# The last 64 tokens of v on 64 partitions, their weights transposed by TensorE

## The chip, the core and the metric

The kernel runs on one core of a Trainium2 chip. The metric is the device time of one execution in microseconds (us), as the median of several runs. The engines are TensorE (PE, with its weight loads shown apart as PEld), VectorE (DVE), ScalarE (ACT), GpSimd (POOL) and SyncE (SP), which issues nearly all transfers.

## The reference, cut to what matters

There are 8 batches of 8 heads, 576 tokens and a head size of 64. For each head 32 packed queries `p` attend to all 576 keys `k` and values `v`; the packed result then serves as keys and values for the 576 real queries. Two expert layers follow on 4608 tokens (512 to 1536 to 512, then 512 to 1024 to 1024 to 512), all in 32-bit floats.

```python
def sm_attn(qq, kk, vv):
    s = scale * np.matmul(qq, kk.transpose(0, 1, 3, 2))
    s = s - np.max(s, axis=-1, keepdims=True)
    a = np.exp(s)
    a = a / (np.sum(a, axis=-1, keepdims=True) + 1e-09)
    return np.matmul(a, vv)
p_packed = sm_attn(p, k, v)
out = sm_attn(q, p_packed, p_packed)
```

The change touches the first of the two calls alone, in its last part: exp, the transposes of its result (the weights of the sum over tokens), and the product with `v`.

## The kernel before, in words

The first call is worked in 16 units. Unit `u` is four heads of one batch, so that its 4 x 32 packed queries fill 128 partitions. The work of a unit is spread over four steps of a loop that runs by hand-written order (line 625): in step `s` the kernel transposes the keys of unit `s` (`pa_kT`), makes the scores of unit `s - 1` (`pa_s`) and their exp (`pa_exp`), transposes the exp of unit `s - 2` (`pa_T`), multiplies it by `v` for unit `s - 3` (`pa_P`), and transposes the finished result of unit `s - 4` (`pa_PT`). Every engine takes its instructions in this order. Between them stand, at chosen quarter steps, the first pieces of the second call (`q_rows` to `q_aT`), of the weight conversion (`w_conv`, `raw_load`) and of the first expert layer (`c_mm`, `stage1`). From line 897 on the expert layers follow, in which TensorE works almost without a break.

The 576 tokens of `v` are taken in two parts. The first 512 (`TM`) come in one transfer for each unit, four neighbouring tokens to a partition (`vm`, line 497), so that partition `p` holds tokens `4 p` to `4 p + 3`. The last 64 (`TR`) come for four units at once (`load_vr`, line 480), in four transfers, one for each head of a unit: head `hq` lies on partitions `32 hq` to `32 hq + 31`, two neighbouring tokens to a partition.

The scores lie in PSUM as 2 x 288: the even tokens in the first half, the odd ones in the second, and in each half in an order that comes from the transposes of the keys. `pa_exp` reads them so and writes `a` as 2 x 288, in order of tokens within each half. `pa_T` picks for `r` from 0 to 3 every second element of a half (`a[:, r % 2, r // 2:256:2]`), which are the tokens `4 p + r`, and TensorE transposes these 128 columns as the weights of an identity product; ACT copies the four results out of PSUM into `apT`. The weights of the last 64 tokens are transposed by DVE, in blocks of 32 x 32 (`apR`, line 548). `pa_P` then sums in one PSUM tile: 16 products over 128 rows, with four heads side by side in four column groups of 32, and after them 8 products over 32 rows, in which head `hq` takes row group and column group `hq`. Line 575 scales the sum by the reciprocal of the exp's sum.

PSUM tiles of two banks (`psum`) go round in three buffers; SP issues the transfers in program order, and an issue waits where its buffer isn't free.

Of the kernel before, what the change touches and what calls it, by code (L numbers as in the profile page):

```python
# [8 lines left out]
F32 = mybir.dt.float32  # L9
# [29 lines left out]
def packed_attention_moe_kernel(  # L39
# [24 lines left out]
    nc = tc.nc  # L64
    B, H, S, D = q.shape
# [4 lines left out]
    HS = S // 2  # L70
    NR = S // 32
    TR = 64
    TM = S - TR
    NV = TM // 128
# [9 lines left out]
    def pool(name, side, bufs=1, **kw):  # L84
        return tc.alloc_tile_pool(name=name, bufs=bufs, side=side, reuse_waits="tile", **kw)
# [25 lines left out]
    ident = const.tile([128, 128], F32, name="ident")  # L111
# [15 lines left out]
    def psum(name):  # L127
        ps_n[0] += 1
        return ps_at[ps_n[0] % len(ps_at)].tile([128, 2, 512], F32, tag="A", name=name)

    def psum1(name):
        return psB.tile([128, 512], F32, tag="B", name=name)
# [4 lines left out]
    hs = [slice(32 * hq, 32 * hq + 32) for hq in range(4)]  # L137
# [329 lines left out]
    pa = pool("pa", "left", bufs=2)  # L467
# [7 lines left out]
    def twice_p(b0, b1):  # L475
        nc.gpsimd.tensor_copy(zp[:, b0:b1, :, 1], zp[:, b0:b1, :, 0])

    vr = pa.tile([128, 2 * B, 2 * D], F32, tag="vr", name="vr", bufs=1)

    def load_vr(u0, u1):  # L480
        for hq in range(4):
            nc.sync.dma_start(
                vr[hs[hq], u0:u1],
                v[u0 // 2:u1 // 2, :, TM:S].rearrange("b (q h) (p r) d -> h p (b q) (r d)", h=4, r=2)[hq])

    def load_k(u):
        if not 0 <= u < 2 * B:
# [46 lines left out]
        return t, mx  # L534

    def pa_exp(u, t, mx):
        a = pa.tile([128, 2, HS], F32, tag="ap", name=f"ap{u}")
        sm = pa.tile([128, 1], F32, tag="sm", name=f"sm{u}", bufs=3)
        nc.scalar.activation(
            a.rearrange("j e (p m) -> j e p m", m=NR // 2),  # L540
            t[:, :, 0:HS].rearrange("j e (m p) -> j e p m", m=NR // 2),
            AF.Exp, bias=mx, scale=scale, accum_out=sm)
        ap_t[u], sm_t[u] = a, sm

    def pa_T(u):
        a, sm = ap_t.pop(u), sm_t[u]
        aR = pa.tile([128, 2, 32], F32, tag="apR", name=f"apR{u}")
        nc.vector.transpose(out=aR, in_=a[:, :, 256:HS])
        nc.vector.tensor_scalar(sm, sm, 1e-9, None, op0=ALU.add)
        nc.vector.reciprocal(sm, sm)  # L550
        t = psum(f"pat{u}")[:, 0]
        for r in range(NV):
            nc.tensor.transpose(
                t[:, 128 * r:128 * r + 128], a[:, r % 2, r // 2:256:2], ident)
        aT = pa.tile([128, NV, 128], F32, tag="apT", name=f"apT{u}")
        pin_at["act"] = nc.scalar.copy(aT, t.rearrange("p (r n) -> p r n", r=NV))
        apT_t[u] = aT, aR

    def pa_P(u):
        vm = kv.pop(("v", u))  # L560
        aT, aR = apT_t.pop(u)
        sm = sm_t.pop(u)
        t = psum1(f"pP{u}")
        for r in range(NV):
            for hq in range(4):
                nc.tensor.matmul(
                    t[hs[hq], 0:64], lhsT=aT[:, r, hs[hq]], rhs=vm[:, hq, D * r:D * r + D],
                    start=(r == 0), stop=False, tile_position=(0, 32 * hq))
        for r in range(2):
            for hq in range(4):  # L570
                nc.tensor.matmul(
                    t[hs[hq], 0:64], lhsT=aR[hs[hq], r], rhs=vr[hs[hq], u, D * r:D * r + D],
                    start=False, stop=(r == 1), tile_position=(32 * hq, 32 * hq))
        Pd = pa.tile([128, 2, 64], F32, tag="Pd", name=f"Pd{u}")
        pin_at["dve"] = nc.vector.tensor_scalar(
            Pd, t[:, 0:64].rearrange("p (o d) -> p o d", o=1).to_broadcast([128, 2, 64]), sm, None, op0=ALU.mult)
        Pd_t[u] = Pd
# [46 lines left out]
    with tc.manual_schedule(engines=M0):  # L624
        for s in range(last + 1):
            if s < U:
                pa_kT(s)
            load_v(s - VD)
            if s == 0 or (s % 4 == 3 and s + 1 < U):
                load_vr(s + (s > 0), s + (s > 0) + 4)  # L630
            load_k(s + KVB)
            run(s, 0)
            run(s, 0.25)
            if 0 <= s - 1 < U:
                x = pa_s(s - 1)
            if 0 <= s - 4 < U:
                pa_PT(s - 4)
            run(s, 0.5)
            if 0 <= s - 2 < U:
                pa_T(s - 2)  # L640
            if 0 <= s - 1 < U:
                pa_exp(s - 1, *x)
            if 0 <= s - 3 < U:
                pa_P(s - 3)
            run(s, 0.75)
# [677 lines left out]
```

## Time and profile before

| what | value |
|---|---|
| timed runs | median 1349.32 us of 3 (1349.02 to 1351.62) |
| the profiled execution | 1353.27 us, of which 1351.4 us are the span from its first to its last instruction |
| busy share of the span | PE 98%, PEld 93%, DVE 54%, ACT 45%, POOL 35% |
| TensorE's granted clock | 0.999 of full, over the span |
| moved by DMA | 278.32 MB, 206 GB/s on average |

The times of the rows further down are those of the profiled execution. A busy TensorE is not TensorE at its peak, because products overlap: the pace of a run of products is read from the length of the run, less that of its last one, divided by their number less one. A wait is put down to the event that ended it.

### The profile page before, as it was taken

The page shows a single profiled execution, that of the slowest core. Times are in us where ns is not written, and L with a number is a line of the kernel's source. Part 1 is how long each engine was busy: PE and PEld are TensorE (multiplying, and loading weights), DVE is VectorE, ACT ScalarE, POOL GpSimd, SP SyncE. Part 2 cuts the span into 40 slices and gives each one's busy share as a digit, 9 for nine tenths or more (in the row PEclk, how much of TensorE's full clock was granted, in tenths as well). Part 3 has the DMA queues.
Part 4 walks back from the last instruction along what each step waited for, and adds up shares of the span by engine and source line. Part 5 has one row for each costly group of instructions (what it writes and reads, how often), then busy time and mean ns, then how long its engine had stood idle before and what let it go on. Part 6 is the DMA issues. An engine that isn't in the chain of part 4 may idle for free.

```text
span 1351.4 us, 26602 instructions
## 1 busy us (share of the span) xinstructions
PE 1328.3 (98%) x10628; PEld 1252.2 (93%) x10628; DVE 731.2 (54%) x1114; ACT 607.6 (45%) x1068; POOL 467.0 (35%) x385
## 2 busy tenths in 40 slices
PE   8889999999999999999999999999999999999999
PEld 6679899999999999999999999889899999999999
DVE  4766877336564466544453389626535535456352
ACT  5774644244443444345554246434344334345241
POOL 1332322323322333244444236305225145153261
PEclk9999999999999999999999999999999999999999
DMA  9976766524445443243453249849769987978855
GB/s 315 343 238 209 214 200 191 168 74 130 148 129 180 121 128 126 71 148 120 142 153 117 81 162 337 292 151 346 250 226 309 313 296 269 318 258 277 315 203 172
DMA packets 192348, 278.32 MB, mean 206 GB/s; under 512 B 71008, under 2 KB 124256, under 8 KB 189920
## 3 DMA queue, kind: packets, MB, share of 16 engines
q1 hardware_dynamic: 192224, 276.62, 63.0%
q8 instruction: 84, 1.38, 0.4%
q14 instruction: 40, 0.33, 0.1%
HBM read 217.84 MB, written 58.72 MB: 205 GB/s over the span
## 4 chain that ended last, share of the span: by engine, by line
PE 81%; DMA 4%; DVE 3%; ACT 1%; issue 0%; SPq 0%; DVEq 0%; ACTq 0%
PE px L675 20%; PE pA L1111 14%; PE pg L446 10%; PE pv L446 9%; PE pB L1111 7%; PE po L1201 5%; PE poA L1225 4%; PE pC L1111 3%; PE pw L767 3%; PE poB L1225 3%; PE pc L413 2%; DMA x2r<-X2d 1%; DMA out_dram<-kA 1%; PE psq L210 1%; DVE x2T L843 1%
## 5 line engine op out<-in xcount | busy, mean ns | idle before, releaser
L89 POOL TENSOR_TENSOR ul<-u,uh 128x576 fp32r<-128x576 f32 x96 | 145.9, 1520 | 303.8 <-ACT uh L96 281.9
L675 PE MATMUL px<-uh,woh 128*128 128x384 f32 x576 | 147.7, 337 | 0.2
L675 PE MATMUL px<-ul,woh 128*128 128x384 f32 x576 | 146.3, 334 | 0.0
L675 PE MATMUL px<-uh,wol 128*128 128x384 f32 x576 | 146.3, 334 | 0.0
L455 DVE TENSOR_TENSOR u<-u,pv 128x576 f32<-128x576 f32 x96 | 71.9, 750 | 135.3 <-PE pv L446 119.3
L687 DVE TENSOR_TENSOR acc<-acc,px 128x768 f32<-128x768 f32 x72 | 68.1, 950 | 85.1 <-PE px L675 84.6
L96 ACT CAST uh<-u 128x576 fp32r<-128x576 f32 x96 | 64.6, 674 | 103.5 <-DVE u L455 103.1
L89 POOL TENSOR_TENSOR wol<-wof,woh 128x512 fp32r<-128x512 f32 x48 | 65.3, 1370 | 126.7 <-ACT woh L96 121.6
L675 PEld LDWEIGHTS px<-uh,woh 128*128 128x128 f32 x576 | 102.5, 188 | 6.0 <-issue 3.3
L451 ACT ACTIVATE u<-pg 128x576 f32<-128x576 f32 x96 | 62.6, 652 | 96.6 <-PE pg L446 90.7
L675 PEld LDWEIGHTS px<-uh,wol 128*128 128x128 f32 x576 | 104.1, 188 | 0.0
L675 PEld LDWEIGHTS px<-ul,woh 128*128 128x128 f32 x576 | 104.1, 188 | 0.0
L446 PE MATMUL pg<-aTh,ch 128*128 128x288 f32 x384 | 83.9, 300 | 1.2 <-DVE cl L89 0.8
L446 PE MATMUL pv<-aTh,ch 128*128 128x288 f32 x384 | 82.8, 297 | 0.9 <-DVE cl L89 0.6
L446 PE MATMUL pg<-aTh,cl 128*128 128x288 f32 x384 | 82.3, 296 | 0.5 <-DVE cl L89 0.5
L446 PE MATMUL pg<-aTl,ch 128*128 128x288 f32 x384 | 82.4, 296 | 0.0
L446 PE MATMUL pv<-aTh,cl 128*128 128x288 f32 x384 | 82.1, 295 | 0.0
L446 PE MATMUL pv<-aTl,ch 128*128 128x288 f32 x384 | 82.1, 295 | 0.0
L446 PEld LDWEIGHTS pg<-aTh,ch 128*128 128x128 f32 x384 | 63.0, 188 | 9.3 <-DVE u L455 3.2
L89 DVE TENSOR_TENSOR cl<-pc,ch 128x1024 fp32r<-128x1024 f32 x48 | 56.6, 1216 | 26.2 <-ACT ch L425 26.2
L446 PEld LDWEIGHTS pv<-aTh,ch 128*128 128x128 f32 x384 | 61.7, 188 | 2.0 <-DVE cl L89 0.8
L446 PEld LDWEIGHTS pg<-aTh,cl 128*128 128x128 f32 x384 | 61.9, 189 | 0.7 <-DVE cl L89 0.7
(415 smaller groups left out, 3443.5 us busy)
## 6 DMA issues: line engine op xcount, KB each, us to landing
wsp<-wsd SPq DMA_DIRECT2D x112, 512.0 KB, 4.3
wf<-Wd SPq DMA_DIRECT2D x36, 512.0 KB, 5.7
wob<-wobd SPq DMA_DIRECT2D x18, 1024.0 KB, 7.1
wsd<-ws SPq DMA_DIRECT2D x56, 256.0 KB, 3.2
ws<-wsd SPq DMA_DIRECT2D x49, 256.0 KB, 5.2
wob<-wobd SPq DMA_DIRECT2D x40, 256.0 KB, 5.6
km<-in_k_dram SPq DMA_DIRECT2D x16, 576.0 KB, 7.3
wof<-wod SPq DMA_DIRECT2D x36, 256.0 KB, 2.8
```

Source lines behind the costliest of these rows:

```text
L89: x = eng.tensor_tensor(out=out, in0=src, in1=hi.bitcast(F32), op=ALU.subtract)
L96: nc.scalar.copy(hi, src)
L413: nc.tensor.matmul(t[hs[at], b, Q], lhsT=PTd[es, 2 * (2 * P + b) + Q, hs[hq]], rhs=w[es, 2 * Q + hq // 2].rearrange("p g n -> p (g n)"), s ...
L446: nc.tensor.matmul(t[:, hf, 0:HS], lhsT=w[:, b % 2, Q, cols], rhs=x[:, Q, hf, :], start=first, stop=last,)
L451: x = nc.scalar.activation(u, t[:, :, 0:HS], AF.Silu)
L455: x = nc.vector.tensor_tensor(out=u, in0=u, in1=t[:, :, 0:HS], op=ALU.mult)
L675: nc.tensor.matmul(t[:, h, 0:CW], lhsT=w[:, 128 * d:128 * d + 128], rhs=x[:, CW * c:CW * c + CW], start=first, stop=last,)
L687: pin_at["acc"] = nc.vector.tensor_tensor(out=o, in0=o, in1=t[:, :, 0:CW], op=ALU.add)
L767: nc.tensor.matmul(t[:, 1], lhsT=a[:, kk], rhs=w, start=(i == 0), stop=(i == 11))
L1111: nc.tensor.matmul(bk[n], lhsT=w[:, hl, 128 * d:128 * d + 128], rhs=r[:, d], start=(first and d == 0 and i == 0), stop=(d == 1 and i == 2) ...
L1201: nc.tensor.matmul(t, lhsT=a[:, j, cols], rhs=w[:, f], start=first, stop=last)
L1225: nc.tensor.matmul(bk[n][m], lhsT=l, rhs=w[i][:, h], start=(first and i == 0 and q == 0), stop=(i == NPB - 1 and q == 2), skip_group_check ...
```

## The change

The last 64 tokens of `v` come in one transfer for four units instead of four: 64 partitions, one token to a partition, all heads beside each other. Exp writes `a` as one row of 576 in order of tokens, so that even tokens are written in steps of two elements, and odd ones likewise. The four sources of TensorE's transposes are then `a[:, r:512:4]`, and the last 64 columns are a fifth source, transposed by TensorE into the second bank of the same PSUM tile and copied out by DVE, where DVE made the transpose itself. The 8 products over 32 rows become 4 over 64 rows, all on the first 64 rows of the array, one for each column group.

```diff
-    vr = pa.tile([128, 2 * B, 2 * D], F32, tag="vr", name="vr", bufs=1)
+    vr = pa.tile([TR, 8 * B, D], F32, tag="vr", name="vr", bufs=1)
     def load_vr(u0, u1):
-        for hq in range(4):
-            nc.sync.dma_start(
-                vr[hs[hq], u0:u1],
-                v[u0 // 2:u1 // 2, :, TM:S].rearrange("b (q h) (p r) d -> h p (b q) (r d)", h=4, r=2)[hq])
+        nc.sync.dma_start(
+            vr[:, 4 * u0:4 * u1], v[u0 // 2:u1 // 2, :, TM:S].rearrange("b h p d -> p (b h) d"))
...
-        a = pa.tile([128, 2, HS], F32, tag="ap", name=f"ap{u}")
+        a = pa.tile([128, S], F32, tag="ap", name=f"ap{u}")
...
-            a.rearrange("j e (p m) -> j e p m", m=NR // 2),
+            a.rearrange("j (p m e) -> j e p m", m=NR // 2, e=2),
...
-        aR = pa.tile([128, 2, 32], F32, tag="apR", name=f"apR{u}")
-        nc.vector.transpose(out=aR, in_=a[:, :, 256:HS])
...
-        t = psum(f"pat{u}")[:, 0]
+        t2 = psum(f"pat{u}")
+        t = t2[:, 0]
         for r in range(NV):
             nc.tensor.transpose(
-                t[:, 128 * r:128 * r + 128], a[:, r % 2, r // 2:256:2], ident)
+                t[:, 128 * r:128 * r + 128], a[:, r:TM:NV], ident)
+        nc.tensor.transpose(t2[0:TR, 1, 0:128], a[:, TM:S], ident)
+        aR = pa.tile([TR, 128], F32, tag="apR", name=f"apR{u}")
+        nc.vector.tensor_copy(aR, t2[0:TR, 1, 0:128])
...
-        for r in range(2):
-            for hq in range(4):
-                nc.tensor.matmul(
-                    t[hs[hq], 0:64], lhsT=aR[hs[hq], r], rhs=vr[hs[hq], u, D * r:D * r + D],
-                    start=False, stop=(r == 1), tile_position=(32 * hq, 32 * hq))
+        for hq in range(4):
+            nc.tensor.matmul(
+                t[hs[hq], 0:64], lhsT=aR[:, hs[hq]], rhs=vr[:, 4 * u + hq],
+                start=False, stop=True, tile_position=(0, 32 * hq))
```

## Rows read from the trace of the kernel before

**Rows 1.** The page, parts 1 and 4: busy time; the chain's shares by engine.

```profile
PE 1328.3 (98%) x10628; PEld 1252.2 (93%) x10628; DVE 731.2 (54%) x1114; ACT 607.6 (45%) x1068; POOL 467.0 (35%) x385
...
PE 81%; DMA 4%; DVE 3%; ACT 1%; issue 0%; SPq 0%; DVEq 0%; ACTq 0%
```

**Rows 2.** Windows: length, then busy us of PE, PEld, DVE, ACT, POOL; clock; DMA.

```profile
12.00:86.00 74.00, 66.88 (x1320) 47.59 (x1322) 52.40 (x141) 56.88 (x109) 18.43 (x14) 1.00 1.00 320
86.00:150.00 64.00, 62.65 (x638) 56.33 (x635) 40.95 (x63) 38.04 (x57) 20.29 (x14) 1.00 0.68 206
150.00:770.00 620.00, 618.52 (x5119) 586.14 (x5118) 328.89 (x418) 267.22 (x381) 216.39 (x150) 1.00 0.46 137
```

**Rows 3.** Waits of PE, 12 to 95 us: sum, times, longest (us).

```profile
PE pPT L581 <- DVE Pd L575: 1.4, 1, 1.4
PE pP L566 <- ACT kT L516: 1.2, 2, 0.8
PE pkr L514 <- issue: 1.0, 1, 1.0
PE pat L553 <- DVE qT L180: 0.8, 2, 0.6
PE pg L446 <- DVE cl L89: 0.8, 1, 0.8
PE pP L566 <- issue: 0.6, 1, 0.6
```

**Rows 4.** Timeline of PE, 36 to 46 us: start, length (us), instructions merged.

```profile
38.08 0.64 PE L553 MATMUL pat<-ident,ap 128*128 128x128 f32 x4
38.65 0.65 PE L566 MATMUL pP<-vm,apT 128*32 128x64 f32 x32
39.23 0.42 PE L571 MATMUL pP<-vr,apR 32*32 32x64 f32 x16
39.59 1.09 PE L511 MATMUL pk<-ident,km 128*128 128x128 f32 x8
...
41.96 1.06 PE L177 MATMUL pqT<-ident,qr 128*128 128x128 f32 x8
```

**Rows 5.** Weight loads of two lines: ns min/median/max, first and last start (us).

```profile
L553 PEld LDWEIGHTS pat<-ident,ap x64: 194/207/218, 13.1 to 85.5; 128*128 128x128 f32 x64
...
L511 PEld LDWEIGHTS pk<-ident,km x128: 137/141/231, 5.4 to 74.4; 128*128 128x128 f32 x128
```

**Rows 6.** ACT's groups by form, whole span: busy us, mean ns, idle before.

```profile
L96 ACT CAST uh<-u 128x576 fp32r<-128x576 f32 x96 | 64.6, 674 | 103.5 <-DVE u L455 103.1
...
L96 ACT CAST woh<-wof 128x512 fp32r<-128x512 f32 x48 | 29.6, 620 | 72.2 <-PE px L675 50.7 <-DVE wof L354 15.2 <-DMA wof<-wod 6.1
...
L350 ACT ACTIVATE wf<-raw_w 128x512 f32<-128x512 f32 x24 | 15.4, 676 | 2.5 <-DMA raw_w<-in_moe_w_gate_dram 2.5
...
L539 ACT ACTIVATE ap<-psp,mx 128x576 f32<-128x576 f32 x16 | 11.9, 746 | 5.0 <-DVE mx L533 3.6 <-PE pk L511 1.4
...
L96 ACT CAST w3h(0, 0)_7494<-w3T(0, 0)_7492 128x512 fp32r<-128x512 f32 x1 | 1.2, 1165 | 0.7 <-DVE w3T(0, 0)_7492 L750 0.7
```

**Rows 7.** Groups by form, 0 to 95 us: busy us, mean ns, idle before.

```profile
L96 ACT CAST aTh<-aT 128x576 fp32r<-128x576 f32 x4 | 5.1, 1286 | 0.0
...
L548 DVE STREAM_TRANSPOSE apR<-ap 128x64 f32<-128x64 f32 x16 | 3.8, 235 | 0.0
...
L181 DVE COPY qT<-pqr 128x128 f32<-128x128 f32 x4 | 1.1, 280 | 0.0
```

**Rows 8.** DMA, 0 to 110 us: queue's packets, MB, share; issues, KB, us to landing.

```profile
q1 hardware_dynamic: 27280, 31.27, 89.8%
...
vr<-in_v_dram SPq DMA_DIRECT2D x16, 64.0 KB, 7.9
```

**Rows 9.** Timeline of SP, 53 to 60 us.

```profile
54.16 4.53 SPq L482 DMA_DIRECT2D vr<-in_v_dram  x4
```

**Rows 10.** Waits of ACT, 12 to 95 us: sum, times, longest (us).

```profile
ACT wf L350 <- DMA raw_w<-in_moe_w_gate_dram: 2.5, 1, 2.5
```

## The prediction

> **What bounds the kernel now.** I read the page's busy shares first: TensorE is busy for 98% of the span, and the chain that ended last is 81% TensorE [rows 1]. The view by windows then splits the span. From 150 to 770 us TensorE stands still for 1.5 us in 620; between 12 and 86 us, where the sixteen units of the packed attention run, it is busy 66.88 of 74 us, ACT 56.88, DVE 52.40, and the DMA engines are full (share 1.00) [rows 2]. So what the change does to these 74 us moves everything behind them, and what it does to TensorE there is the first thing to count: only 74 - 66.88 = 7.1 us of idle time can swallow it. The view of waits says how that idle time is cut up: six kinds of wait with a longest one of 0.6 to 1.4 us, ended by DVE, ACT or issue [rows 3]. None of the six is ended by a DMA.
>
> **The change part by part**, per unit, then times 16.
>
> *Products over the last tokens.* Eight products become four. Each stands in the trace as two records, four column groups running side by side, so 16 records are 4 rounds and become 2. The 32 records before them make 8 rounds: (0.65 - 0.22) / 7 = 0.061 us a round; the rounds to be cut give (0.42 - 0.21) / 3 = 0.07 [rows 4]. I take 2 x 0.061 = 0.12 us, 2.0 us in all; bounds 2.2 us saved and nothing saved (should the entry into the 64-row shape cost more than the one into the 32-row shape: entry now takes about 0.15 us against a round of 0.061: the last of the eight rounds begins at 38.65 + 7 x 0.061 = 39.08, the next at 39.23 [rows 4]).
>
> *One more transpose.* Its source, the last 64 columns, is contiguous. Contiguous 128-column transposes follow each other at (1.06 - 0.27) / 7 = 0.113 us [rows 4]; 16 of them are +1.8 us. Below: half of it, for 64 columns (0.9). Above: 0.113 and a change of array shape, 0.15 - 0.06 = 0.09 more (3.3).
>
> *The other four transposes.* Exp now writes in token order, so their sources step by four floats (16 bytes) where they stepped by two (8 bytes). This is the one large unknown, for no weight load of the trace steps that far. What it shows: the load of a contiguous 128-column block takes 141 ns, at 8-byte steps 207 ns [rows 5], and four such transposes follow each other at (0.64 - 0.28) / 3 = 0.12 us, or 0.94 ns a column [rows 4]. ACT shows farther steps. Its contiguous casts take 674 ns for 576 elements and 620 for 512, so (674 - 620) / 64 = 0.84 ns an element and 190 ns beside; the cast that reads in 512-byte steps takes 1165 ns, (1165 - 190) / 512 = 1.90 an element; the activation that reads every second word (8-byte steps) 676 ns, 0.95 [rows 6]; the cast that writes in 72-byte steps 1286 ns, again (1286 - 190) / 576 = 1.90 [rows 7]. Far steps cost 1.90, 8-byte steps half of that, on ACT as on the weight load (0.94). At 16 bytes the price is therefore between 0.94 (nothing added) and 1.90. I take 1.90: contiguous to 8 bytes has already lengthened the load, and another halving of the density lands on the far end. A transpose then comes every 1.90 x 128 = 0.24 us, 0.12 more than now; 64 of them are +7.7 us. Bounds: 0, and 0.24 + 0.11 = 0.35 us each if load and product stop overlapping (+14.7).
>
> The Trainium skill, "SBUF — State Buffer", section "Specifications (TRN2)", has 16-byte lines that want two hits each for full speed; two floats 8 bytes apart share a line and two 16 bytes apart don't, which is the price taken (the trace agrees on ACT's far steps, 1.90 against 0.84). But the same page, section "Door 1: The DMA port swizzle", says of stepping for free: "4 fp32". And "TensorE: Matmul & The Clock Gate", section "LDWEIGHTS (loading the stationary operand)", makes the load a matter of columns alone, about 107 ns for 128; the trace's 141 and 207 for the same 128 columns don't agree. By either sentence this edit costs nothing and the time is that of rival B.
>
> *DVE.* A 235 ns transpose goes, a copy out of PSUM comes: the 128x128 one takes 280 ns [rows 7], so +0.045 us a unit, 0.7 us in all, on an engine idle for a fifth of the stretch: nothing. The copy now waits for the fifth transpose, and behind it on DVE stands the scaling of the unit before, which waits for products that TensorE makes after these transposes anyway; the products that read the copy come a step later. Cover gone: 0.28 us a unit, 4.5 us. ACT's copy of the weights may wait for the fifth transpose too, 0.11 us, counted above.
>
> *Exp.* Writes in 8-byte steps: by the 0.95 above at most 0.11 x 576 = 0.06 us on 746 ns [rows 6], 1.0 us over 16 on an ACT with 17 us idle; I let 0.3 us through. Bounds: 0, and as the 72-byte write, (1.90 - 0.84) x 576 = 0.61 us each, 9.8 us on ACT.
>
> *Loads.* Four transfers become one, four times. The bytes stay (16 x 64 KB), the pieces go from 512 to 256 bytes. A vr transfer takes 7.9 us to land in a full queue [rows 8]; no wait of TensorE in [rows 3] is for one. I cost the transfer at nothing, with bounds in C and E below. On SP twelve issues go; four of them held it 4.53 us [rows 9], but what is behind them are loads of k and raw weights, and the only long DMA wait in the stretch is one of ACT, 2.5 us [rows 10].
>
> *Sum.* TensorE: 7.7 + 1.8 - 2.0 = +7.5 us, 0.47 a unit. How much of it reaches the end? The waits of [rows 3] are ended by ACT or DVE work that itself follows TensorE's work of the step before, so most idle time moves along; a wait can swallow one step's 0.47 us only if it is longer, and six such kinds are there: 6 x 0.47 = 2.8. Through come 7.5 - 2.8 = 4.7, with exp's 0.3 makes 5.0 us. The bounds of this step are 0.4 (all 7.1 us of idle time used) and 7.5. The profiled execution took 1353.27 us (span 1351.4 and 1.9 around it), 3.9 above the median of the timed runs; it would become 1358.3, the median 1349.3 + 5.0 = 1354.3 us.
>
> **The rivals.**
> A (forecast): the 16-byte step doubles the load. 1354.3, own range +2.5 to +7.7: 1351.8 to 1357.0.
> B: the step costs nothing, the load still hides at 0.12 us. TensorE gets 1.8 - 2.0 = -0.2 us: 1349.1, between -1.3 and +1.3. For it: 8-byte steps moved the pace of the transposes only from 0.113 to 0.12 us [rows 4], and if words are fetched in pairs, a 16-byte step fetches no more than an 8-byte one. Against it: ACT's 1.90 at far steps, twice its 0.95.
> C, the other side: faster. Place: SP's queue from 54.16 us on. With B's transposes (at best 0.9 - 2.0 = -1.1 us) and three of four issues gone (4.53 us become about 1.1), the raw weights start some 3 us sooner and ACT's wait of 2.5 us for them vanishes: -1.1 - 2.5 = -3.6, 1345.7. It decides only if that wait holds TensorE up; against it stands that none of TensorE's six is ended by a DMA.
> D: exp's writes cost as the 72-byte ones, 9.8 us on ACT, which has 17.1 us idle; with A's 5.0 and some 4 us of it showing, 1358.3. For it: the 72-byte write is the only strided write of ACT among the rows; against it: 0.95 at 8-byte reads.
> E: the queue. 1.05 MB of vr, at 31.27 MB in 89.8% of 110 us [rows 8], is 3.3 us of the queue; twice that if the halved pieces go at half the rate, +3.3 us on what waits for loads, with A 1357.6. Against it: no wait of TensorE on a DMA.
>
> **How the numbers follow.** A 0.58, B 0.20, C 0.12, D 0.06, E 0.04. What a measurement of this kernel can tell from no change is about 0.2%, 2.7 us. Slower by more: nearly all of A (0.54), D and E: 0.64. Within: the rest of A, B, a little of C: 0.26. Faster: 0.10. The range takes in A and B with its lower bound, and D and E in their middle: 1348.0 to 1358.5; left out are most of C, the upper ends of D and E, and the end of A's price where nothing overlaps.
>
> **What would show it.** Right: weight loads of pat at 300 ns or more, and four strided transposes spaced 0.24 us; the last unit's group, at 85.5 us now [rows 5], starting 4 to 5 us later, and the first products of the next stage as much later; the rounds over the last tokens two instead of four. Wrong: transposes still 0.12 us apart (then B); exp above 0.85 us (D); TensorE waiting for k, v or the last tokens of v (E). If the transposes do take 0.24 us but the stretch ends less than 2 us later, the step that fails is the share let through.

## The result, and the profile after

| | median | runs | ratio to before, 95% interval |
|---|---|---|---|
| before | 1349.17 us | 4 (1348.68 to 1351.62) | |
| after | 1359.95 us | 4 (1358.40 to 1361.45) | 1.0077 [1.0062, 1.0092] |

By the ratio the change costs 0.77%, 10.4 us; the two medians differ by 10.8. The profiled execution of after took 1358.40 us (span 1356.6), only 5.1 us more than that of before. The two profiles differ by more than that where the change is. First line L350's conversions of raw weights on ACT (duration in ns min/median/max, first and last start), before and then after:

```profile
L350 ACT ACTIVATE wf<-raw_w x24: 654/674/707, 50.4 to 201.1; 128x512 f32<-128x512 f32 x24
...
L350 ACT ACTIVATE vt_w<-raw_w x16: 657/669/697, 592.0 to 735.4; 128x512 f32<-128x512 f32 x16
```

```profile
L350 ACT ACTIVATE wf<-raw_w x24: 664/674/713, 52.4 to 211.6; 128x512 f32<-128x512 f32 x24
...
L350 ACT ACTIVATE vt_w<-raw_w x16: 661/672/707, 602.4 to 745.8; 128x512 f32<-128x512 f32 x16
```

At 201 us after is 10.5 us behind, at 735 us 10.4: all is lost in the packed attention and what overlaps it, nothing in the 500 us behind it. What the profile of before lost later is its own: from 870 to 880 us its clock is 0.83 (in after it is full there), and from 1050 to 1110 us its TensorE stands still for 2.26 of 60 us, where after has no idle time. By windows (length, then busy us of PE, PEld, DVE, ACT, POOL; granted clock; DMA share; GB/s), before and then after:

```profile
1050.00:1110.00 60.00, 57.74 (x411) 57.27 (x410) 28.12 (x47) 21.87 (x47) 14.93 (x15) 1.00 0.89 306
```

```profile
1050.00:1110.00 60.00, 60.00 (x427) 60.00 (x426) 29.06 (x48) 22.75 (x48) 17.11 (x18) 1.00 0.92 323
```

So I read the mechanism in the first 100 us and take the sizes from the timed runs. The windows of after that answer to the first two of [rows 2], and three short ones:

```profile
12.00:86.00 74.00, 63.03 (x1090) 44.00 (x1089) 47.56 (x130) 48.77 (x96) 15.20 (x12) 0.93 1.01 308
86.00:150.00 64.00, 58.89 (x609) 51.18 (x615) 38.54 (x60) 34.91 (x56) 18.91 (x13) 0.95 0.63 187
```

```profile
50.00:60.00 10.00, 7.50 (x121) 4.86 (x121) 7.18 (x16) 5.36 (x10) 2.89 (x2) 0.66 1.06 372
70.00:80.00 10.00, 6.91 (x84) 5.01 (x84) 6.69 (x16) 5.80 (x10) 1.75 (x1) 0.83 0.88 288
90.00:100.00 10.00, 7.53 (x114) 6.03 (x106) 3.98 (x10) 4.36 (x9) 0.79 (x1) 0.66 0.33 82
```

Every engine is less busy between 12 and 86 us than before: PE 63.03 of 74 us (66.88 before), DVE 47.56 (52.40), ACT 48.77 (56.88). No engine became the bound: they wait, and since after falls behind, less of the work lies in these 74 us. The granted clock, full all through these stretches in before, is 0.66 from 50 to 60 us.

What the forecast rested on is not there. The weight loads of the transposes that step by 16 bytes, and the fifth one; then TensorE's timeline of a step (start, length, instructions merged):

```profile
L550 PEld LDWEIGHTS pat<-ident,ap x64: 195/211/229, 11.5 to 93.8; 128*128 128x128 f32 x64
...
L552 PEld LDWEIGHTS pat<-ident,ap x16: 113/124/173, 12.0 to 94.0; 128*64 128x64 f32 x16
```

```profile
38.17 0.65 PE L550 MATMUL pat<-ident,ap 128*128 128x128 f32 x4
38.65 0.27 PE L552 MATMUL pat<-ident,ap 128*64 128x128 f32 x1
39.24 0.65 PE L566 MATMUL pP<-vm,apT 128*32 128x64 f32 x32 [0.31 <-ACT kT L514]
39.82 0.32 PE L570 MATMUL pP<-vr,apR 64*32 64x64 f32 x8
40.07 1.09 PE L509 MATMUL pk<-ident,km 128*128 128x128 f32 x8
```

The load takes 211 ns (207 in [rows 5]), the four transposes 0.65 us (0.64 in [rows 4]), so one comes every (0.65 - 0.28) / 3 = 0.12 us, as before. The last of them starts at 38.17 + 0.65 - 0.28 = 38.54, and the fifth 0.11 us later. From the first product over the last tokens to the next work it is 40.07 - 39.82 = 0.25 us (before 39.59 - 39.23 = 0.36).

What is new stands in ACT's waits, and in TensorE's (12 to 95 us: sum, times, longest):

```profile
ACT apT L556 <- DVE apR L554: 18.8, 14, 2.9
ACT wf L350 <- DMA raw_w<-in_moe_w_gate_dram: 4.6, 1, 4.6
```

```profile
PE pk L509 <- ACT apT L556: 3.6, 2, 1.9
PE pP L570 <- issue: 1.7, 1, 1.7
```

ACT's copy of the transposed weights, which in before waited 3.4 us in all for TensorE, waits 18.8 us for DVE's copy of the fifth transpose. The two read the same PSUM tile, DVE its second bank and ACT its first, and the program puts DVE's first; the wait goes by the tile. How long DVE takes to get there, after the fifth transpose (38.65 + 0.27 = 38.92 us), DVE's timeline shows, and ACT's beside it:

```profile
38.04 0.75 DVE L247 TENSOR_REDUCE qsm<-sT 128x18 f32<-128x576 f32 x1 [1.44 <-ACT sT L242]
...
39.22 0.69 DVE L530 TENSOR_REDUCE mx<-psp 128x1 f32<-128x576 f32 x1
39.95 0.15 DVE L531 TENSOR_SCALAR mx<-mx 128x1 f32<-128x1 f32 x1
40.02 0.14 DVE L545 TENSOR_SCALAR sm<-sm 128x1 f32<-128x1 f32 x1
40.20 0.16 DVE L546 RECIPROCAL sm<-sm 128x1 f32<-128x1 f32 x1
40.28 0.26 DVE L554 COPY apR<-pat 64x128 f32<-64x128 f32 x1
```

```profile
39.06 0.29 ACT L581 COPY PTd<-pPT 128x128 f32<-128x128 f32 x1
40.63 0.59 ACT L556 COPY apT<-pat 128x512 f32<-128x512 f32 x1 [1.28 <-DVE apR L554]
41.12 0.79 ACT L537 ACTIVATE ap<-psp,mx 128x576 f32<-128x576 f32 x1
```

ACT is free from 39.06 + 0.29 = 39.35 us and starts at 40.63. The exp of the next unit, behind the copy on ACT, starts at 41.12, though DVE had its maximum ready at 39.95 + 0.15 = 40.10.

The second new thing is in the DMA queue, which was full before too. Packets of the stretch from 12 to 70 us, and the loads of k in it (KB each, median us from issue to landing), before and then after:

```profile
DMA packets 14477, 19.71 MB, mean 340 GB/s; under 512 B 2023, under 2 KB 12428, under 8 KB 14466
...
km<-in_k_dram SPq DMA_DIRECT2D x11, 576.0 KB, 8.5
```

```profile
DMA packets 15169, 18.99 MB, mean 327 GB/s; under 512 B 4967, under 2 KB 13126, under 8 KB 15160
...
km<-in_k_dram SPq DMA_DIRECT2D x10, 576.0 KB, 10.7
```

With all 16 engines busy in both, the packets under 512 bytes go from 2023 to 4967, the queue moves 327 GB/s in place of 340, and a load of k takes 10.7 us to land in place of 8.5. One transfer of vr lands after 11.4 us (64 KB ones took 7.9 in [rows 8]). The first raw gate weight lands at 52.3 us, before at 50.4; ACT waits 4.6 us for it.

The time to landing of k has to be read with care, because it counts from the issue, and SP is held in another place now. Around the third group of vr SP's timeline shows, before and then after:

```profile
34.80 4.50 SPq L482 DMA_DIRECT2D vr<-in_v_dram  x4
40.47 0.35 SPq L491 DMA_DIRECT2D km<-in_k_dram  x1
```

```profile
35.34 1.74 SPq L481 DMA_DIRECT2D vr<-in_v_dram  x1
37.17 4.72 SPq L489 DMA_DIRECT2D km<-in_k_dram  x1
```

In before the four issues of vr hold SP, in after the one of k behind them does. That load of k lands 8.5 us after its issue in before and 13.5 in after; counted from the first issue of vr it is 14.2 us (40.47 + 8.5 - 34.80) against 15.3 (37.17 + 13.5 - 35.34). At the fourth group it is 13.4 against 13.8. So of the longer landing 1.1 and 0.4 us are lateness.

### The profile page after: what moved, and what is told of

Same layout as the page of the kernel before. It is cut to its first block, busy times and chain, and to the rows that moved or that the text cites. A ratio compares the mean times of both kernels' runs of the same rounds, so it can differ in the third digit from the quotient of the medians.

```text
span 1356.6 us, 26356 instructions
## 1 busy us (share of the span) xinstructions
PE 1329.4 (98%) x10516; PEld 1252.3 (92%) x10516; DVE 734.3 (54%) x1114; ACT 606.9 (45%) x1068; POOL 465.8 (34%) x385
## 4 chain that ended last, share of the span: by engine, by line
PE 79%; DVE 4%; DMA 3%; issue 1%; ACT 0%; SPq 0%; DVEq 0%; ACTq 0%
PE px L674 20%; PE pA L1110 12%; PE pg L446 10%; PE pv L446 9%; PE pB L1110 6%; PE poA L1224 5%; PE po L1200 4%; PE poB L1224 4%; PE pw L766 3%; PE pC L1110 3%; PE pc L413 2%; DVE ws L89 1%; DMA w12r<-w12d 1%; PE psq L210 1%; DMA wobd<-wobs 0%
## 5 line engine op out<-in xcount | busy, mean ns | idle before, releaser
L96 ACT CAST woh<-wof 128x512 fp32r<-128x512 f32 x48 | 29.7, 620 | 75.3 <-PE px L674 50.6
```

What stands on the lines that cost most here:

```text
L96: nc.scalar.copy(hi, src)
```

## The experiments

Ratios are to the kernel before, timed on the same chip; its median was 1348.55 to 1349.84 us in all of them. A ratio is not the quotient of the two medians and differs from it by up to 0.0008; costs in us are worked out from the ratios.

**Is the 16-byte step free?** The kernel before, with exp in token order and the transposes' sources in steps of four floats; products and loads as before; DVE's transposes stay and read every second element.

```diff
-            a.rearrange("j e (p m) -> j e p m", m=NR // 2),
+            a.rearrange("j (p m e) -> j e p m", m=NR // 2, e=2),
...
-        nc.vector.transpose(out=aR, in_=a[:, :, 256:HS])
+        nc.vector.transpose(out=aR, in_=a[:, TM:S].rearrange("j (p e) -> j e p", e=2))
...
-                t[:, 128 * r:128 * r + 128], a[:, r % 2, r // 2:256:2], ident)
+                t[:, 128 * r:128 * r + 128], a[:, r:TM:NV], ident)
```

> The kernel before with one part of the change: exp writes in token order and the four sources of TensorE's transposes step by four floats; the last 64 tokens stay with DVE's transpose (reading in 8-byte steps), 8 products and four transfers. Theory W: 1348 to 1351, transposes 0.12 us apart, exp near 790 ns. Theory P, if it is the exp (48 ns x 16) and the steps: 1352 to 1356. Theory L: as before, 1349.

1349.93 us, 0.9998 [0.9988, 1.0009]: nothing. The loads take 211 ns, the transposes come every 120 to 122 ns. This half of the change is free.

**Does ACT's copy behind DVE's cost the time?** The changed kernel with ACT's copy put ahead of DVE's:

```diff
-        aR = pa.tile([TR, 128], F32, tag="apR", name=f"apR{u}")
-        nc.vector.tensor_copy(aR, t2[0:TR, 1, 0:128])
         aT = pa.tile([128, NV, 128], F32, tag="apT", name=f"apT{u}")
         pin_at["act"] = nc.scalar.copy(aT, t.rearrange("p (r n) -> p r n", r=NV))
+        aR = pa.tile([TR, 128], F32, tag="apR", name=f"apR{u}")
+        nc.vector.tensor_copy(aR, t2[0:TR, 1, 0:128])
```

> The changed kernel with one swap: ACT's copy of the four transposed blocks is issued before DVE's copy of the fifth, so that ACT waits for TensorE and DVE for ACT, not ACT for DVE. Theory W (ACT's copy stands behind DVE's whole queue, 20.4 us of waits, and TensorE starves behind it): ACT's wait for apR is gone, the granted clock stays at full in the front, 1346 to 1351 us. Theory P (the new work itself, the fifth transpose and the slower exp, costs the time): 1357 to 1361, as changed. Theory L (the one transfer on 64 partitions in 256-byte pieces holds the loads up): 1357 to 1361.

1355.06 us, 1.0032 [1.0020, 1.0044]. Now DVE's copy waits for ACT's, 2.1 us in all. ACT's waits in it:

```profile
ACT wf L350 <- DMA raw_w<-in_moe_w_gate_dram: 5.4, 1, 5.4
...
ACT apT L554 <- PE pat L552: 4.2, 9, 1.3
```

The other way round, the kernel before with that wait alone: DVE copies one column of the PSUM tile ahead of ACT's copy, for no use.

```diff
+        touch = pa.tile([128, 1], F32, tag="touch", name=f"touch{u}")
+        nc.vector.tensor_copy(touch, t[:, 0:1])
```

> The kernel before with the suspected wait alone: after the reciprocal, DVE copies one column of the PSUM tile of the transposes into an unused tile, ahead of ACT's copy of that tile. Nothing else is changed. Theory W: ACT's copy waits for DVE as in the changed kernel, TensorE's clock falls in places, 1356 to 1362. Theory P and theory L: 1349 to 1350, as before.

1358.03 us, 1.0053 [1.0034, 1.0071], with the same wait in ACT's list:

```profile
ACT apT L558 <- DVE touch L556: 21.1, 15, 2.9
```

And the changed kernel without a copy by DVE: the last 128 columns are the fifth source, ACT copies five blocks at once (712 ns in place of 586), the last tokens of v lie on partitions 64 to 127.

```diff
-        nc.tensor.transpose(t2[0:TR, 1, 0:128], a[:, TM:S], ident)
+        nc.tensor.transpose(t2[:, 1, 0:128], a[:, S - 128:S], ident)
...
+        aT = pa.tile([128, NV + 1, 128], F32, tag="apT", name=f"apT{u}")
+        aR = aT[:, NV]
+        pin_at["act"] = nc.scalar.copy(
+            aT, t2.rearrange("p a (r n) -> p (a r) n", n=128)[:, 0:NV + 1])
...
```

> The changed kernel with the last 128 columns as the fifth source, so that the weights of the last 64 tokens land on partitions 64 to 127 and ACT copies all five blocks in one copy of 640 elements; no copy by DVE; the transfer goes to partitions 64 to 127. Theory W: no wait of ACT for DVE, one more 0.1 us on ACT a unit, 1346 to 1350. Theory P: 1355 to 1360. Theory L: 1357 to 1361, the transfer is as in the changed kernel.

1354.04 us, 1.0031 [1.0016, 1.0047]. Taken away in two ways the wait gives back 0.45% (1.0077 less 1.0032 or 1.0031), 6 us; put alone into the kernel before it costs 0.53%, 7 us. That cause is shown. A fifth transpose in a PSUM tile of its own was not run. Some 4 us remain in both ways, and both still wait for the raw weight (5.4 and 6.9 us).

**Do the loads carry the rest?** First with the loads of v's last tokens nearly gone: in both kernels (the changed one with ACT's copy first) only the first group is loaded, and units 4 to 15 use its values for their last 64 tokens.

```diff
-            if s == 0 or (s % 4 == 3 and s + 1 < U):
+            if s == 0:
...
-rhs=vr[:, 4 * u + hq]
+rhs=vr[:, 4 * (u % 4) + hq]
```

> The changed kernel with ACT's copy first, and only the first of the four groups of v's last tokens loaded: the later units multiply by the first group's tokens (their output is not the reference's). Theory Q: the 4.3 us above the kernel before go, 1346 to 1350, full clock in the front, raw weights land before 50.5 us. Theory P2: 1353 to 1355 as with the loads.

> The kernel before with only the first of the four groups of v's last tokens loaded and used for all units (the output is not the reference's). Control for the changed kernel with few loads. Theory Q: the queue is 0.8 MB shorter, 1346 to 1349. Theory P2: 1349. The difference of the two kernels with few loads is what the change costs or gives without the queue: theory Q says within 1 us, theory P2 4 us.

1344.66 us, 0.9976 [0.9964, 0.9988], and 1346.03 us, 0.9980 [0.9967, 0.9993]. Without the three later groups the two kernels are level, to within some 2.4 us by the intervals. What the changed kernel still loses with ACT's copy first, 0.32% or 4.3 us, hangs on those loads. An engine's added work that shows only while the queue is full is not excluded by this.

**Is it the raw weight?** Its issue one step sooner, ahead of the third group of vr; in the changed kernel with ACT's copy first, in before, and in the changed kernel as it is:

```diff
-RAW0 = (7, 8, 10, 11, 12, 13, 15, 15, 15.5, 16.75)
+RAW0 = (6, 8, 10, 11, 12, 13, 15, 15, 15.5, 16.75)
```

> The changed kernel with ACT's copy ahead of DVE's, and the first raw gate weight issued one step sooner, ahead of the third group of v's last tokens. Theory Q (what is left of the loss is the raw weight landing late behind the longer transfer): the raw weight lands before 50 us instead of 52.2, ACT's wait of 5.4 us for it is gone, TensorE's clock stays full from 50 to 60 us, and the time is 1346 to 1350 us. Rival P (what is left is work on TensorE or DVE): 1353 to 1356 us, whatever the order of the loads.

> The kernel before with the same raw weight issued one step sooner. Theory Q: there only ACT's wait of 2.5 us for the raw weight can go, so 1346 to 1349 us. Rival P: 1349 us, no change.

> The changed kernel as it is (ACT's copy behind DVE's), with the raw weight issued one step sooner. If the two causes (ACT's copy waiting behind DVE's queue; the raw weight's landing) add up, 1354 to 1357 us, about 4 us under the changed kernel. Rival P: 1359 to 1360 us, as the changed kernel.

1354.64 us, 1.0031 [1.0021, 1.0041]; 1349.36, 0.9999 [0.9986, 1.0011]; 1359.13, 1.0067 [1.0053, 1.0080]. Theory Q missed in all three. Rival P's times came out; its reason, work on TensorE or DVE, is what the two runs before these speak against. In the first the raw weight is converted from 46.7 us on, ACT's wait for it is gone and the clock stays full from 50 to 60 us, yet the time is the same. TensorE now waits for the load of k:

```profile
PE pk L509 <- DMA km<-in_k_dram: 1.0, 1, 1.0
```

The same kernel with vr's later groups issued one step later, behind k and the raw weight:

```diff
-            if s == 0 or (s % 4 == 3 and s + 1 < U):
-                load_vr(s + (s > 0), s + (s > 0) + 4)
+            if s == 0:
+                load_vr(0, 4)
             load_k(s + KVB)
...
+            if s % 4 == 0 and 0 < s < U:
+                load_vr(s, s + 4)
```

> The changed kernel with ACT's copy ahead of DVE's, and groups two to four of v's last tokens issued one step later, behind the loads of k and the raw weight of that step. Theory Q: as with the raw weight issued sooner, 1346 to 1351 us, unless the products now wait for the last tokens of v. Rival P: 1353 to 1356 us.

1359.28 us, 1.0069 [1.0055, 1.0083], 5 us worse: now the products wait for vr itself.

```profile
PE pP L570 <- DMA vr<-in_v_dram: 2.6, 2, 2.3
```

So moving one load ahead doesn't help, and moving vr back makes vr late. I read this as a queue in which whatever stands last is late, and the order only chooses which; two orders are not enough to show it.

**Is it the size of the pieces?** The changed kernel with ACT's copy first and other tokens of v in the place of the last ones: as many bytes, 64 partitions and transfers, in pieces of 512 bytes, then of 4 KB (the edit for 512 is shown).

```diff
-            vr[:, 4 * u0:4 * u1], v[u0 // 2:u1 // 2, :, TM:S].rearrange("b h p d -> p (b h) d"))
+            vr[:, 4 * u0:4 * u1].rearrange("p (g t) d -> p g (t d)", t=2),
+            v[u0 // 2:u0 // 2 + 1, :, S - 128:S].rearrange("b h (p t) d -> p (b h) (t d)", t=2))
```

> The changed kernel with ACT's copy ahead of DVE's, whose transfers of v's last tokens (still 64 partitions, 256 KB, one for four units) read 512-byte pieces of other tokens of v in place of 256-byte ones; the values of the last 64 tokens are wrong by that. Theory S (the halved pieces slow the whole full queue): from 12 to 70 us the queue moves 340 GB/s again instead of 326, the raw weight lands by 50.5 us and the time is 1348 to 1351 us. Rival S2 (64 partitions, or one transfer for four units, slow it): 326 GB/s and 1354 to 1356 us.

> As the run with 512-byte pieces, with 4 KB pieces (one for each partition) of other tokens of v, again with wrong values for the last 64 tokens. Theory S: at least as good, 345 GB/s or more from 12 to 70 us, 1345 to 1350 us. Rival S2: 1354 to 1356 us.

1352.68 us, 1.0017 [1.0008, 1.0027], and 1350.59 us, 1.0010 [0.9999, 1.0020], against 1.0032 with 256 bytes. The queue moves 326, 332 and 335 GB/s from 12 to 70 us in the three (256 bytes first), before 340. The kernel before with DVE's useless copy, which runs late as well, moves 341, so the lower rate doesn't come from running late. The packets with 4 KB pieces:

```profile
DMA packets 12639, 19.42 MB, mean 335 GB/s; under 512 B 1870, under 2 KB 10384, under 8 KB 12630
...
km<-in_k_dram SPq DMA_DIRECT2D x10, 576.0 KB, 11.1
```

Larger pieces give 2 to 3 of the 4.3 us back, in order of their size, though the intervals of neighbours overlap. 0.17% [0.08, 0.27], 2.3 us, stay with the piece size of before. A load of k still takes 11.1 us to land with 4 KB pieces, but that says little: in the two kernels with few loads, which are faster than before, it takes 10.3 and 10.2. That the transfer of 256 KB holds up the loads behind it is therefore not shown.

The Trainium skill, "DMA: Bandwidth & Descriptors", section "Specifications", wants 512 bytes or more for full rate; the three rates agree in direction, and 4 KB still adds to 512. The Trainium skill's "SBUF — State Buffer", section "Door 1: The DMA port swizzle", says that 64 partitions are written hardly faster than 32. Before's transfers go to 32 partitions each, so by that sentence the 64 alone would change little; no run here separates it.

**Does the number or size of transfers count in the kernel before?** Twice as many, once with 256-byte pieces and once with 512; then the later groups as 8 and as 4 larger transfers in the place of 12, all with 512-byte pieces.

```diff
+            for r in range(2):            # 256-byte pieces
+                nc.sync.dma_start(vr[hs[hq], u0:u1, D * r:D * r + D], ...)
...
+            for x in (u0, u0 + 2):        # 512-byte pieces
+                nc.sync.dma_start(vr[hs[hq], x:x + 2], ...)
...
+            for at, u0, u1 in ((0, 0, 4), (3, 4, 10), (9, 10, U)):    # 12 transfers
...
+            for at, u0, u1 in ((0, 0, 4), (3, 4, U)):                 # 8 transfers
```

> The kernel before with the loads of v's last tokens cut into 8 transfers a group, one for each head and each of a partition's two tokens: 256-byte pieces, as in the changed kernel, to the same places; nothing else changes. Theory Q (the small pieces lengthen the full load queue, the raw weights land later, ACT and TensorE wait for them): 1352 to 1355, against the next kernel with the same number of transfers 3 us more. Theory P2 (the rest, some 4 us with ACT's copy first, is the work on TensorE and DVE): both 1349 to 1350.

> The kernel before with the same loads cut into 8 transfers a group by halves of the group: 512-byte pieces as before, twice the number of transfers. Control for the one with 256-byte pieces. Theory Q: 1349 to 1351. Theory P2: 1349 to 1350. If SP's issues are what costs, both cut kernels are slower by the same.

> The kernel before with the last 12 units' share of v's last tokens in two groups of six units in place of three of four: 12 transfers in place of 16, the same bytes, the same 512-byte pieces. If the number of transfers is a cost by itself (twice as many cost 7 us), a quarter less gives 1 to 3 us: 1346 to 1348 us. Rival: the time goes by when the raw weight lands, and this moves it little: 1348 to 1351 us.

> The kernel before with all of the last 12 units in one group: 8 transfers in place of 16, 192 KB each in the second group. If the number of transfers counts, 1345 to 1347 us. Rival (a large transfer holds up the loads of k behind it, as the 256 KB one does in the changed kernel): 1350 to 1354 us.

1355.72 us, 1.0046 [1.0029, 1.0062], and 1356.33, 1.0057 [1.0038, 1.0075], with 32 transfers: here the pieces make no difference. The profile shows another picture than in the changed kernel: SP spends 12.19 us on the eight issues of one group, the raw weight behind them is issued at 50.09 us (42.26 in before), and the engines of the queue are no longer always busy. With 512-byte pieces, SP's timeline and the window from 12 to 70 us (DMA share 0.90; before 1.05 and 340 GB/s):

```profile
37.38 12.19 SPq L483 DMA_DIRECT2D vr<-in_v_dram  x8
...
50.09 0.43 SPq L334 DMA_DIRECT2D raw_w<-in_moe_w_gate_dram  x1
```

```profile
12.00:70.00 58.00, 50.81 (x968) 36.38 (x968) 35.99 (x104) 38.45 (x77) 12.31 (x10) 0.91 0.90 301
```

With 12 and 8 transfers: 1350.35 us, 1.0016 [1.0007, 1.0025], and 1351.48 us, 1.0020 [1.0009, 1.0031]. Fewer isn't faster; the 16 of before are the best of the five. With 8 TensorE waits for a load of k, three times as long as in any of the changed kernels, though the queue moves 351 GB/s:

```profile
PE pk L511 <- DMA km<-in_k_dram: 3.0, 1, 3.0
```

**Is a held PSUM tile part of the rest?** With ACT's copy first, DVE's late copy holds the tile, and TensorE waits for it, 0.5 us at a time (once in the first such run, three times with the raw weight sooner). So both copies on ACT, then that with 512-byte pieces of other tokens:

```diff
-        nc.vector.tensor_copy(aR, t2[0:TR, 1, 0:128])
+        nc.scalar.copy(aR, t2[0:TR, 1, 0:128])
```

> The changed kernel with both copies out of the PSUM tile on ACT, the four transposes' first. Theory H (part of what is left is TensorE waiting for a PSUM tile that DVE's late copy still holds, 0.5 us each time): TensorE's waits for that copy are gone; ACT gets 16 short copies more, about 0.25 us each; 1352 to 1354 us, 1 to 3 us below the run with ACT's copy first (1355.06). Rival: the hold is worth nothing, 1355 to 1357 us.

> Both copies on ACT and 512-byte pieces together (wrong values for the last 64 tokens). If ACT's copy behind DVE, the held PSUM tile and the smaller pieces are all of the loss, the kernel is level with the one before or faster: 1345 to 1349.5 us. If something else in the change costs, it stays above 1351 us.

1353.61 us, 1.0030 [1.0018, 1.0042]: no gain over 1.0032 that shows, though ACT has 16 more copies to make. Both together: 1354.23 us, 1.0039 [1.0024, 1.0054]. That missed; by the run with 512-byte pieces alone it should have been some 2 us less. So of the two runs with 512-byte pieces one gained and the other didn't, and only the 4 KB run speaks clearly for the size of the pieces. Why stays open.

## Why the prediction was wrong

The direction was right by luck: the cost that was forecast isn't there, and two that were put at nothing are. 1359.95 us is 1.5 us above the range's upper end. By its steps:

- *The other four transposes*, +7.7 us: failed. "I take 1.90" was the far end of the bounds; the near end, nothing added, is what was measured (0.12 us apart, 211 ns a load; ratio 0.9998 when done alone). ACT's reads at 512-byte steps and writes at 72-byte steps did not carry over to TensorE's weight load at 16 bytes. The argument noted for B, that 8-byte steps had hardly moved the pace, pointed the right way. The sentence of the Trainium skill's "SBUF — State Buffer", section "Door 1: The DMA port swizzle", that lets four fp32 steps be free agrees with this trace as far as the pace goes; the load itself is longer than a contiguous one (211 against 141 ns [rows 5]). The one on two hits to a line (section "Specifications (TRN2)") doesn't, as I read it: 16-byte steps cost 4 ns more than 8-byte ones.
- *One more transpose* (+1.8) and *products* (-2.0): as predicted, 0.11 us added a unit and 0.36 - 0.25 = 0.11 us saved. They cancel. *Exp*: 746 to 794 ns, 0.05 us against the 0.06 expected. *DVE's copy*: 264 ns, 280 expected.
- *DVE*, "nothing": failed, and the largest part of the loss. I called DVE idle for a fifth of the stretch (it is 21.6 of 74 us [rows 2], nearer three tenths) and asked who waits for its copy, and found products a step later. I didn't ask what else reads the same PSUM tile: ACT's copy stands behind DVE's in the program, and so behind all of DVE's queue. The sentence "ACT's copy of the weights may wait for the fifth transpose too, 0.11 us" priced the wrong producer; the wait is 18.8 us in all, 6 us of the time.
- *Loads*, "I cost the transfer at nothing": failed, 4.3 us. Rival E had the place, and with smaller pieces at a lower rate in a full queue probably a part of the mechanism; its size was near too (3.3 us). It got a chance of 0.04, because no wait of TensorE was on a DMA. That was the wrong test: ACT's wait for the raw weight, 2.5 us in before [rows 10], grew to 4.6 us, and a wait of TensorE for k (1.0 us with ACT's copy first and the raw weight sooner) isn't in before. What the 2.3 us are that stay with pieces of 512 bytes is open.
- *Rival C* (faster): SP's four issues of 4.53 us became one of 1.1 us, as C said, but the issue of k behind it took 5.28 us (0.35 in before), so SP gained nothing, and the first raw weight landed 1.9 us later, not sooner.
- *What gets through*: I let idle time swallow 2.8 us of TensorE's extra work. There was no extra work. The loss is waiting, and the six small waits that I read say nothing of a wait that the change itself brings. In the step shown above it holds up ACT's exp, whose maximum was ready 1.0 us before it started.

The two parts, 6.1 us (1.0077 less 1.0032) and 4.3 us (1.0032), make up the 10.4 us because one is got from the other by subtraction. What stands beside that is the first part put alone into the kernel before, 7 us; with 4.3 that is 11.5, within the noise of 10.4. The second part is traced to the loads as a whole. How it divides between the size of the pieces and the rest is not settled.

## What to carry to other kernels

When a copy out of PSUM goes to a second engine, look at everything else that reads that tile: here the engine that was next in the program waited for the whole queue of the one before it, however short the copy was, even one of a single column. Let the engine on the critical chain read first, or not share the tile. In a stretch where the DMA queue is full, a merged transfer isn't free because its bytes are the same: count its pieces, and ask which load stands behind it. And a time to landing counts from the issue: ask first where the issuing engine was held.

## What the runs showed of the hardware

TensorE's clock fell where it had been full. In after it went to the lower of its two levels (1.2 of 2.4 GHz) from 52.2 to 59.0 us, 72.7 to 76.1 and 93.2 to 100.0. TensorE's timeline around the first fall:

```profile
50.58 0.31 PE L570 MATMUL pP<-vr,apR 64*32 64x64 f32 x6
52.63 0.37 PE L570 MATMUL pP<-vr,apR 64*32 64x64 f32 x2 [1.74 <-issue]
53.64 1.94 PE L509 MATMUL pk<-ident,km 128*128 128x128 f32 x8 [0.64 <-PE pP L570]
```

The engine had stood still for 1.74 us with nothing in the profile that ended the wait. The eight transposes of k then take 1.94 us, at full clock 1.09 [rows 4]. What the remaining 4.3 us hang on is not this fall: with the raw weight sooner it is gone, and the kernel is no faster (1.0031 against 1.0032).

What makes that idle stretch of 1.7 us is not known. In four changed kernels it stands before the same product, the last one over the last tokens of a unit, with the copies and the raw weight in different order: 1.74 us here, 1.69 with ACT's copy first, 1.38 with one copy, 1.84 with the raw weight sooner (but 0.21 with ACT's copy first and the raw weight sooner). That points at a place in TensorE's program, not at one load; no run tests it. All such waits of TensorE from 12 to 95 us come to 1.6 us in before, 2.8 with ACT's copy first, and 0.8 and 0.9 in the kernels with few loads; but with ACT's copy first and the raw weight sooner they are 1.4 and the kernel is no faster, so by themselves they don't explain the 4.3.

The third fall, which is not there with ACT's copy first, does cost time in after. Between 93.2 and 100.0 us TensorE is busy for 6.74 of 6.80 us, at half the clock. The same two groups of products, before and then after:

```profile
87.18 0.43 PE L446 MATMUL pg<-aTl,ch 128*128 128x288 f32 x2
87.45 0.43 PE L446 MATMUL pg<-aTh,cl 128*128 128x288 f32 x2
```

```profile
97.99 0.68 PE L446 MATMUL pg<-aTl,ch 128*128 128x288 f32 x2
98.47 0.68 PE L446 MATMUL pg<-aTh,cl 128*128 128x288 f32 x2
```

They follow each other at 0.27 and at 0.48 us. The last transposes of the weights start at 93.8 us, 8.3 later than in before (85.5 [rows 5]); the last products over the last tokens start at 100.3, 10.8 later (89.5). So some 2.5 us of what ACT's wait cost in this execution came through the clock.
